# Weight gathers held over a phase border, multiplications tied to their own phase, and a new order of attention's steps

## The chip, the core and the metric

The kernel runs on one core of a Trainium2 chip. That core has five engines, which run their own instruction rows and wait for each other by semaphores: TensorE (PE, matrix products), VectorE (DVE), ScalarE (ACT), GpSimd (POOL) and SyncE (SP), and 16 DMA engines that move data between memory (HBM) and the core's two on-chip memories. The metric is the time of one execution on the device, in microseconds (us), as the median of several executions.

## What is computed

Three layers follow each other; x has 2304 rows of 512 numbers.

```python
# attention: B=4, H=8, S=576, D=64; heads 0-3 a local mask (32 back), heads 4-7 a strided one
scores = where(mask, q @ k.T / sqrt(D), -1e9); scores -= max(scores)
attn = exp(scores); attn /= sum(attn) + 1e-9
x = attn @ v
# layer one: 8 experts, all of them on all rows, weighted by a Sinkhorn-normalized gate
out = sum(P[:, e:e+1] * (relu(x @ w1[e]) @ w2[e]) for e in range(8))   # w1 512x1024, w2 1024x512
# layer two: each row goes to one expert, 288 rows at most to each, best logits first
for e in range(8):
    mask = assigned == e
    out[mask] = relu(x[mask] @ w1[e]) @ w2[e]
```

## The kernel before

Every float32 product is made of float16 products of a high and a low part, three for each, so each weight matrix exists as a high and a low piece.

**Attention** is 32 steps, numbered 0 to 31, each a part of a few heads. A step passes through S (scores, TensorE), M (row maximum and its scale, VectorE, L404 and L405), E (exponential and row sum, ScalarE, L418), N (normalization: `den` on VectorE, L427 and L428, the product on GpSimd), T (transposes, TensorE), O (product with v, TensorE, L459) and X (split of the result into high and low part, ScalarE and VectorE). A string `ORDER`, written by hand, names these parts one after the other: `S0 M0 ... O31`. Between them stand single letters that advance other work by one step: `s` is a side chain that begins with the scale of v (its first four steps are the reductions `vmx`, L343, two for each load `vl` and `vs` of v; then `amax`, `vall`, `vscale`), `W` and `V` prepare the first weights of layer one (`wmx` L527, splits on ScalarE L547 and VectorE L548), `L` and `Y` load q, k and v, `R` loads raw weights, `G`, `H` and `C` belong to the gate and the routing, and `Q` is one unit of layer one's first expert on TensorE (L662, L680). In this stage each engine runs its instructions in the order of that string. The unit `Q` first appears behind X7.

**Layer one** follows from 326 to 1360 us, and to 1594.8 its last expert together with the logits and the first routing of layer two.

**Layer two** has eight phases, one for each expert, written in the function `ffn`. A phase has eight f-units (first matrix, 12 matmuls of 288 columns, L1736), each followed by relu and copy on ScalarE (L1741, L1742: `h2h`) and a split on VectorE (L1743: `h2l`), and then four d-units (second matrix, 24 matmuls, L1786), whose result ScalarE copies to `yt`. Beside that four things are done for the phase that comes next:

- `search`: the cut of the routing is found in steps. VectorE compares (L1379), TensorE counts (`pcnt`, L1385), VectorE compares the count (L1387), TensorE sums (`pany`, L1391), VectorE takes the step (L1394). These steps stand in TensorE's row between the matmuls.
- `load_w2` gathers the next expert's weights in four pieces of 1 MB (numbered 0 to 3: first matrix high and low, second matrix high and low) by indirect DMAs that GpSimd issues (L1608). Three sets of buffers rotate. They lie in old tiles, so that a piece may be called `acc`, `xh`, `xl`, `w1s`, `w2h` or `w2l` in the trace; its source is `wd`. Each piece is tied by a semaphore to the newest ScalarE copy (`self.copied`), which spreads the pieces over the phase: `part(n)` lets one go when at least `GAP` = 3 units have passed.
- `ffn_g` gathers the 288 rows of x in three gathers of 96 (`g`, L1625), also from GpSimd's queue, once the place of each row is known (d = 1). For phases 1 to 5 SyncE then issues three DMA transposes (`xg`, L1639); in the others TensorE transposes. The first f-unit of the next phase needs `xg`.
- `ffn_osc` multiplies one column of the gathered rows by the routing's weight, three operations of 96 x 1 on VectorE (`osc`, L1649). They are written at f = 4 of the phase that uses the rows; `ffn_y`, which multiplies the result, needs them at that phase's end.

In this layer only TensorE runs in the order as written (`MAN2 = {ET.PE}`). On the other engines a scheduler places an instruction where its operands are due, so it can stand earlier than it is written.

## Time and profile before

| | us |
|---|---|
| median of 3 runs (lowest, highest) | 1857.66 (1850.5, 1863.44) |
| the profiled execution | 1857.89 |
| its span on the chip | 1856.1 |
| busy: PE, DVE, ACT, POOL | 1786.5 (96%), 1126.2, 908.0, 550.6 |

The span is the time from the first to the last instruction of the profiled execution; 1.8 us lie outside of it. Phases of layer two are named by number: phase p starts with its first matmul of L1736, at 1594.76, 1629.43, 1664.11, 1698.46, 1730.03, 1764.80, 1793.19 and 1819.06 us; "1 to 2" is the end of phase 1, where the x rows and weights of phase 2 are fetched. A wait in the profile is the time in which an engine stood still ahead of an instruction, put down to what came last.

### The profile page before, as it was taken

The page shows a single profiled execution, that of the slowest core. Times are in us where ns is not written, and L with a number is a line of the kernel's source. Part 1 is how long each engine was busy: PE and PEld are TensorE (multiplying, and loading weights), DVE is VectorE, ACT ScalarE, POOL GpSimd, SP SyncE. Part 2 cuts the span into 40 slices and gives each one's busy share as a digit, 9 for nine tenths or more (in the row PEclk, how much of TensorE's full clock was granted, in tenths as well). Part 3 has the DMA queues.
Part 4 walks back from the last instruction along what each step waited for, and adds up shares of the span by engine and source line. Part 5 has one row for each costly group of instructions (what it writes and reads, how often), then busy time and mean ns, then how long its engine had stood idle before and what let it go on. Part 6 is the DMA issues. An engine that isn't in the chain of part 4 may idle for free.

```text
span 1856.1 us, 33029 instructions
## 1 busy us (share of the span) xinstructions
PE 1786.5 (96%) x12789; PEld 1087.5 (59%) x12789; DVE 1126.2 (61%) x2706; ACT 908.0 (49%) x2147; POOL 550.6 (30%) x557
## 2 busy tenths in 40 slices
PE   6899999999999999999999999999999999889897
PEld 5666765555455545555555555555546764667786
DVE  5744448767766475646646664677545658767640
ACT  5555533572476347545735654467635540223243
POOL 2121203141343044213413231233355622223341
PEclk8899999999999999999999999999999999999999
DMA  8121012233375047404751553355541213466661
GB/s 266 40 71 41 26 46 80 80 131 120 121 245 191 16 155 249 137 35 159 236 155 52 185 164 106 136 199 173 173 137 45 47 46 117 126 154 197 192 198 61
DMA packets 116561, 237.16 MB, mean 128 GB/s; under 512 B 48620, under 2 KB 53300, under 8 KB 108180
## 3 DMA queue, kind: packets, MB, share of 16 engines
q1 hardware_dynamic: 108724, 192.05, 32.4%
q0 software_dynamic: 7680, 43.01, 6.9%
q8 instruction: 100, 1.64, 0.4%
q14 instruction: 57, 0.47, 0.1%
HBM read 160.75 MB, written 64.50 MB: 121 GB/s over the span
## 4 chain that ended last, share of the span: by engine, by line
PE 57%; issue 15%; DVE 14%; DMA 6%; ACT 5%; POOL 3%; SPq 0%; POOLq 0%; ACTq 0%; DVEq 0%
PE l L1104 22%; PE l L1160 15%; PE l L680 7%; PE l L662 4%; PE mm L1736 3%; DVE w1s L548 2%; PE mm L1786 2%; POOL raw L1013 2%; DMA g<-xd,raw 2%; ACT sm L418 1%; DMA raw<-in_moe_w_dram 1%; DVE w1s L1379 1%; DVE wmx L1060 1%; PE po L459 1%; PE ps L393 1%
## 5 line engine op out<-in xcount | busy, mean ns | idle before, releaser
L1104 PEld LDWEIGHTS <-w1s 128*128 128x128 f16 x3864 | 370.1, 98 | 210.9 <-issue 4.2
L1104 PE MATMUL l<-sx,w1s 128*128 128x384 f16 (+2 forms) x2208 | 337.3, 312 | 1.3 <-ACT vV L1119 1.1
L1160 PE MATMUL l<-w2h,hl 128*128 128x512 f16 x864 | 327.5, 379 | 0.0
L1160 PE MATMUL l<-w2l,hh 128*128 128x512 f16 x864 | 327.5, 379 | 0.0
L1160 PE MATMUL l<-w2h,hh 128*128 128x512 f16 x864 | 327.5, 379 | 0.0
L552 POOL TENSOR_TENSOR m2l<-raw,m2h 128x512 f16<-128x512 f32 x176 | 206.0, 1172 | 395.7 <-ACT raw L551 340.6
L1160 PEld LDWEIGHTS <-hh 128*128 128x128 f16 x1728 | 167.7, 98 | 197.4
L1104 PE MATMUL l<-xh,w1s 128*128 128x384 f16 (+2 forms) x1104 | 258.7, 312 | 3.5 <-DVE hl L952 2.0
L712 DVE SCALAR_TENSOR_TENSOR acc<-l,pe,acc 128x512 f32<-128x512 f32 x126 | 94.2, 749 | 174.2 <-PE l L1160 150.7
L1013 POOL TENSOR_TENSOR raw<-raw 128x256 f32<-128x256 f32 x112 | 100.6, 901 | 324.2 <-DVE w1s L548 244.9
L1060 DVE TENSOR_REDUCE wmx<-raw 128x1 f32<-128x512 f32 x240 | 152.0, 678 | 43.8 <-DMA raw<-in_moe_w_dram 41.7
L1104 PE MATMUL l<-xl,w1s 128*128 128x384 f16 (+2 forms) x552 | 171.3, 312 | 0.0
L550 ACT ACTIVATE m2h<-raw,wscale 128x512 f16<-128x512 f32 x176 | 125.3, 712 | 86.0 <-DVE wscale L288 29.0
L1160 PEld LDWEIGHTS <-hl 128*128 128x128 f16 x864 | 84.5, 98 | 101.9
L1119 ACT ACTIVATE vV<-l 128x384 f32<-128x384 f32 x144 | 68.3, 487 | 133.2 <-PE l L1104 132.3
L551 ACT ACTIVATE raw<-raw,wscale 128x512 f32<-128x512 f32 x176 | 127.0, 722 | 5.7
L680 PE MATMUL l<-w2h,hl 128*128 128x512 f16 x288 | 109.8, 381 | 0.0
L680 PE MATMUL l<-w2l,hh 128*128 128x512 f16 x288 | 109.8, 381 | 0.0
L680 PE MATMUL l<-w2h,hh 128*128 128x512 f16 x288 | 109.8, 381 | 0.0
L429 POOL TENSOR_TENSOR sm<-sm,den 96x768 f32<-96x768 f32 (+1 forms) x32 | 42.7, 1333 | 190.2 <-DVE den L428 118.8
L548 DVE SCALAR_TENSOR_TENSOR w1s<-raw,wscale,w1s 128x512 f16<-128x512 f32 x96 | 82.5, 904 | 17.3 <-ACT w1s L547 17.3
L547 ACT ACTIVATE w1s<-raw,wscale 128x512 f16<-128x512 f32 x96 | 57.8, 658 | 71.8 <-POOL raw L1013 53.9
(399 smaller groups left out, 3009.1 us busy)
## 6 DMA issues: line engine op xcount, KB each, us to landing
raw<-in_moe_w_dram SPq DMA_DIRECT2D x120, 512.0 KB, 5.7
sx<-sd SPq DMA_DIRECT2D x15, 1536.0 KB, 7.4
wd<-m2h SPq DMA_DIRECT2D x64, 256.0 KB, 3.6
wd<-m2l SPq DMA_DIRECT2D x64, 256.0 KB, 3.4
kq<-in_qk_dram SPq DMA_DIRECT2D x16, 592.0 KB, 3.9
sd<-sx SPq DMA_DIRECT2D x3, 1536.0 KB, 5.6
acc<-in_moe_w_dram SPq DMA_DIRECT2D x2, 2048.0 KB, 10.3
w1s<-wl SPq DMA_DIRECT2D x4, 896.0 KB, 5.7
```

What stands on the lines that cost most here:

```text
L548: nc.vector.scalar_tensor_tensor(lo, raw, s, hi, op0=OP.mult, op1=OP.subtract)
L550: nc.scalar.activation(hi, raw, AF.Copy, scale=s)
L551: nc.scalar.activation(raw, raw, AF.Copy, scale=s)
L552: nc.gpsimd.tensor_tensor(lo, raw, hi, op=OP.subtract)
L662: nc.tensor.matmul(ps, l[:, d, fs], r[:, d, t0:t0 + nb], start=k == 0, stop=k == 3 * DC - 1)
L680: nc.tensor.matmul(ps, l[:, f, js], r[:, f], start=k == 0, stop=k == 3 * FC - 1)
L712: self.last = [nc.vector.scalar_tensor_tensor(a, ps, pe[:, c:c + 1], a, op0=OP.mult, op1=OP.add).ins]
L1013: nc.gpsimd.tensor_tensor(o, x, y, op=OP.subtract)
L1060: nc.vector.tensor_reduce(mx[:, 2 * q + k:2 * q + k + 1], part(q)[:, k * 512:k * 512 + 512], axis=AX.X, op=OP.max, apply_absolute_value=True)
L1104: self.nc.tensor.matmul(ps, self.w1s[:, fs, x, k, d], a[y][:, d], start=first and m == 0, stop=m == 5, skip_group_check=not first)
L1119: copy = lambda o, i: nc.scalar.activation(o, i, AF.Copy)
L1160: nc.tensor.matmul(ps, l[:, f, js], r[:, f], start=k == 0, stop=k == 3 * FC - 1)
```

## The change

1. The string `ORDER` has the same parts in another order. At the start S0 and M0 now stand ahead of the first `s`; three `s` stand together ahead of E1; the last `W` ahead of the first unit moves from before T6 to behind X7. Later the exchanges are small.
2. `att_consts` makes ScalarE compute the exponential of one column of ones (`warm`), which nobody reads.
3. Each osc multiplication gets a dependency without a semaphore (it only binds the scheduler) on the `h2l` split of f = 4 of its own phase.
4. `ffn` keeps a list of (phase, piece). What is left of it when the d-units begin is let go there only if it belongs to this phase, or is piece 0 or 1 of the next one, except for one that may go at d = 0; the rest is held over and let go in the f-units of the next phase. Where the next phase's list is made early (f of 3 or less), `GAP` stays 3, else it is 2. The fourth piece of every phase from 1 to 7 thus comes behind the copy of f = 0 of its own phase; before, it was tied to a d-unit or the last f-unit of the phase before. In phases 5 to 7 the pieces 0, 1 and 2 are tied to the units f = 3, 6 and 7 of the phase before, where it was 0, 3 and 6.

```diff
-ORDER = ("s S0 M0 S1 s M1 E0 N0 E1 S2 M2 W s N1 s s L T0 s S3 M3 s E2 s N2 s s S4 M4 O0 W E3 L X0 T1 N3 S5 W W M5 O1 W "
+ORDER = ("S0 M0 S1 s M1 E0 s s s E1 S2 N0 M2 W L N1 s T0 E2 S3 O0 L s s M3 s s S4 s N2 M4 W E3 R X0 T1 N3 S5 W W M5 O1 W "
...
-         "E8 N8 W X5 W T6 O6 X6 T7 s O7 L X7 Q S9 M9 Y Q s E9 Q s T8 s L Q Q s N9 V S10 M10 s Q O8 V V E10 X8 Q T9 Q "
+         "N8 W X5 T6 L O6 X6 s T7 s O7 X7 W Q Q S9 M9 Y s Q T8 E9 s Q L Q Q s N9 V S10 M10 s s Q s O8 V V E10 Q T9 X8 "
...
+        warm = self.asm.tile([128, 1], F32, name="warm")
+        nc.scalar.activation(warm, self.onesf[:, 0:1], AF.Exp)
...
         for s in range(3):
-            self.nc.vector.tensor_tensor(self.fx[ph][1][:, s:s + 1], self.gs[ph][s][:, 2 * DM:].bitcast(F32),
-                                         self.places[ph][1][:96], op=OP.mult)
+            st = self.nc.vector.tensor_tensor(self.fx[ph][1][:, s:s + 1], self.gs[ph][s][:, 2 * DM:].bitcast(F32),
+                                              self.places[ph][1][:96], op=OP.mult)
+            self.tc.add_manual_dep(st.ins, self.split.name, mybir.DependencyInfo(
+                mybir.DependencyClass.NoSync, mybir.DependencyReason.DATA), reason="later")
...
-        parts, since = [], 0
+        parts, since, gap = [], 0, GAP
...
-            if parts and since >= GAP:
-                self.load_w2(ph + 1, (parts.pop(0),), self.copied)
+            if parts and since >= gap:
+                p, k = parts.pop(0)
+                self.load_w2(p, (k,), self.copied)
                 since = 0
...
-                nc.vector.tensor_tensor(hl[:, f], r, hh[:, f], op=OP.subtract)
+                self.split = nc.vector.tensor_tensor(hl[:, f], r, hh[:, f], op=OP.subtract).ins
...
-                        parts, since = list(range(4)), GAP
+                        since = since if parts else GAP
+                        gap = GAP if f <= GAP else GAP - 1
+                        parts += [(ph + 1, k) for k in range(4)]
                         loaded = True
                 part(1)
             yt = self.fy[ph] = fp.tile([128, DC, CAP], F32, name="yt")
+            while parts and parts[0][0] == ph:
+                part(GAP)
             for d in range(DC):
-                part(2)
+                if not d or parts and parts[0][1] < 2:
+                    part(2)
+                else:
+                    since += 2
...
-            while parts:
+            while parts and parts[0][1] < 2:
                 part(GAP)
```

The row of VectorE at the program's start, before and then after (`vmx` is the reduction of v, `mx` the row maximum of a step, `den` the row sums, `wmx` a maximum of the weights):

```order
L310 CAST identb<-identf 128x128
L343 TENSOR_REDUCE vmx<-vl 128x1
L404 TENSOR_REDUCE mx<-ps 96x2x3
L405 TENSOR_SCALAR mx<-mx 96x2x3
L343 TENSOR_REDUCE vmx<-vl 128x1
L404 TENSOR_REDUCE mx<-ps 96x2x3
L405 TENSOR_SCALAR mx<-mx 96x2x3
L427 TENSOR_SCALAR den<-den 96x2x3
L428 RECIPROCAL den<-den 96x2x3
```

```order
L312 CAST identb<-identf 128x128
L406 TENSOR_REDUCE mx<-ps 96x2x3
L407 TENSOR_SCALAR mx<-mx 96x2x3
L345 TENSOR_REDUCE vmx<-vl 128x1
L406 TENSOR_REDUCE mx<-ps 96x2x3
L407 TENSOR_SCALAR mx<-mx 96x2x3
L345 TENSOR_REDUCE vmx<-vl 128x1
L345 TENSOR_REDUCE vmx<-vs 72x1 x2
L429 TENSOR_SCALAR den<-den 96x2x3
L430 RECIPROCAL den<-den 96x2x3
```

The first row maximum now stands ahead of the reduction of v that waits for the load, and all four reductions stand ahead of the first `den`, where it was two.

The row of GpSimd's queue in phase 4, before and then after; `wd_73` to `wd_76` are the sources of pieces 0 to 3, and the `w1s`, `w2h` and `w2l` rows are the pieces for phase 5:

```order
L1608 DMA w1s<-wd_73,raw_3214 128x4096
L1704 DMA out_dram<-y,raw_3214 2304x512 x2
L1608 DMA w1s<-wd_74,raw_3214 128x4096
L1704 DMA out_dram<-y,raw_3214 2304x512
L1608 DMA w2h<-wd_75,raw_3214 128x4096
L1608 DMA w2l<-wd_76,raw_3214 128x4096
L1625 DMA g_18957<-xd,raw_3214 96x1026
L1625 DMA g_18959<-xd,raw_3214 96x1026
L1625 DMA g_18961<-xd,raw_3214 96x1026
```

```order
L1610 DMA acc<-wd_76,raw_3216 128x4096
L1708 DMA out_dram<-y,raw_3216 2304x512 x2
L1610 DMA w1s<-wd_73,raw_3216 128x4096
L1708 DMA out_dram<-y,raw_3216 2304x512
L1610 DMA w1s<-wd_74,raw_3216 128x4096
L1610 DMA w2h<-wd_75,raw_3216 128x4096
L1627 DMA g_18958<-xd,raw_3216 96x1026
L1627 DMA g_18960<-xd,raw_3216 96x1026
L1627 DMA g_18962<-xd,raw_3216 96x1026
L1610 DMA w2l<-wd_76,raw_3216 128x4096
```

The fourth piece for phase 5 (`w2l`) moved behind the three x gathers, and the fourth piece for phase 4 (`acc<-wd_76`) now opens the phase.

The row of VectorE in the second matrix of phase 4, before, and then of VectorE in the first matrix of phase 5, after; the `jt` rows and those with `pcnt` and `pany` are the search:

```order
L1379 SCALAR_TENSOR_TENSOR w1s<-w1s,zero,jt_2445 128x400
L1379 SCALAR_TENSOR_TENSOR w1s<-w1s,zero,jt_2445 128x320
L1649 TENSOR_TENSOR osc<-g_18957,raw_3214 96x1
L1387 TENSOR_SCALAR w1s<-pcnt,sx 128x40
L1649 TENSOR_TENSOR osc<-g_18959,raw_3214 96x1
L1394 TENSOR_SCALAR w1s<-pany,zero 128x40
L1649 TENSOR_TENSOR osc<-g_18961,raw_3214 96x1
```

```order
L1748 TENSOR_TENSOR h2l<-h_19253,h2h 128x288
L1553 TENSOR_TENSOR sx<-w1s,raw_3216 128x864
L1492 CAST raw_3216<-raw_3216 128x2
L1748 TENSOR_TENSOR h2l<-h_19284,h2h 128x288
L1651 TENSOR_TENSOR osc<-g_18958,raw_3216 96x1
L1651 TENSOR_TENSOR osc<-g_18960,raw_3216 96x1
L1651 TENSOR_TENSOR osc<-g_18962,raw_3216 96x1
```

The three osc rows of phase 5 left the search steps of phase 4 and stand in phase 5, behind a split.

## Rows read from the trace of the kernel before

**Rows 1.** Windows by stage: stretch, length, busy us (instructions), granted clock, DMA share, GB/s

```profile
58.00:253.00 195.00, 192.11 (x1960) 135.35 (x1960) 92.79 (x236) 104.94 (x442) 36.76 (x38) 0.97 0.13 43
...
326.00:1360.00 1034.00, 1029.85 (x5627) 541.27 (x5628) 654.24 (x1216) 570.60 (x1069) 314.32 (x292) 1.00 0.45 148
...
1594.80:1841.10 246.30, 229.37 (x2403) 186.33 (x2403) 135.92 (x619) 83.52 (x185) 69.14 (x70) 0.97 0.57 166
```

**Rows 2.** Windows by half phase of layer two (first, second matrix)

```profile
1609.30:1629.43 20.13, 16.38 (x211) 13.10 (x209) 11.77 (x49) 2.49 (x6) 5.55 (x6) 1.00 0.82 233
1629.43:1643.13 13.70, 13.70 (x130) 11.37 (x131) 12.13 (x64) 7.69 (x17) 4.98 (x5) 1.00 0.39 121
1643.13:1664.11 20.98, 15.93 (x212) 12.88 (x209) 11.04 (x39) 2.49 (x6) 5.14 (x5) 0.96 0.89 209
...
1680.55:1698.46 17.91, 16.08 (x216) 13.09 (x212) 10.14 (x37) 2.24 (x6) 4.96 (x5) 1.00 0.84 231
...
1712.21:1730.03 17.82, 15.88 (x212) 13.01 (x210) 9.35 (x34) 2.08 (x5) 5.29 (x5) 1.00 0.75 224
...
1743.73:1764.80 21.07, 16.93 (x212) 13.64 (x209) 9.51 (x36) 2.08 (x5) 4.49 (x5) 0.92 0.72 186
```

**Rows 3.** Waits of TensorE in layer two: us in total, times, longest

```profile
PE pany L1391 <- DVE w1s L1387: 7.6, 5, 4.1
PE pcnt L1385 <- DVE w1s L1379: 4.0, 8, 0.9
PE mm L1736 <- DMA xg<-g: 3.9, 1, 3.9
```

**Rows 4.** Waits of VectorE in layer two, same columns

```profile
DVE osc L1649 <- DMA g<-xd,raw: 23.3, 14, 5.2
```

**Rows 5.** Timeline, phase 4: start, us, engine, line, operation, [idle <- releaser]

```profile
1748.29 0.92 POOL L1625 DMA_INDIRECT g<-xd,raw  x1 [2.16 <-DVE raw L1561]
...
1756.77 0.16 DVE L1649 TENSOR_TENSOR osc<-g,raw 96x1 f32<-96x1 f32 x1 [5.22 <-DMA g<-xd,raw]
```

**Rows 6.** The three x gathers of phase 4 to 5, by tile g

```profile
DMA to landing us min/median/max: 7.7/8.1/8.5
```

**Rows 7.** The three x gathers of phase 1 to 2, by tile g

```profile
DMA to landing us min/median/max: 3.1/3.4/4.1
```

**Rows 8.** Timeline of GpSimd's queue, phase 1

```profile
1653.21 0.96 POOL L1608 DMA_INDIRECT w2l<-wd,raw  x1 [0.30 <-issue]
```

**Rows 9.** The three transposes of phase 1 to 2, by tile xg

```profile
L1639 SPq DMA_TRANSPOSE xg<-g x3: 1212/1213/1914, 1652.5 to 1655.4; - x3
...
DMA to landing us min/median/max: 4.1/8.6/9.4
```

**Rows 10.** Transposes of 2 to 3 and 3 to 4, by tile xg

```profile
DMA to landing us min/median/max: 2.7/3.3/3.9
```

**Rows 11.** Windows behind TensorE's two longest stops, columns as in rows 1

```profile
1662.30:1669.10 6.80, 4.99 (x38) 3.35 (x39) 1.51 (x8) 0.85 (x2) 0.00 (x0) 0.50 0.14 27
1757.90:1761.30 3.40, 3.40 (x32) 2.41 (x30) 1.26 (x4) 0.00 (x0) 0.00 (x0) 0.50 1.07 121
```

**Rows 12.** Timeline at the program's start, all engines

```profile
6.79 1.60 PE L393 MATMUL ps<-kq 64*96 64x128 f32 x12 [1.86 <-DMA kq<-in_qk_dram]
...
12.86 0.95 DVE L343 TENSOR_REDUCE vmx<-vl 128x1 f32<-128x768 f32 x1 [11.09 <-DMA vl<-in_vl_dram]
...
14.96 1.28 ACT L418 ACT_TABLE_LOAD   x1 [14.96 <-DVE mx L405]
...
16.25 0.36 ACT L418 ACTIVATE sm<-ps,mx 96x128 f32<-96x128 f32 x1
```

**Rows 13.** Window of attention's first steps, columns as in rows 1

```profile
24.40:52.20 27.80, 20.61 (x272) 16.81 (x272) 24.47 (x57) 26.32 (x125) 10.21 (x9) 0.92 0.68 220
```

**Rows 14.** Timeline of TensorE, first unit of layer one

```profile
57.96 0.40 PE L662 MATMUL l<-xh,w1h 128*128 128x256 f16 x1
```

**Rows 15.** The weight gathers of layer two, by line L1608

```profile
DMA to landing us min/median/max: 5.7/7.1/9.4
```

More of the change, by code (lines that the diff above doesn't have):

```diff
@@ L30 @@
 KQ_BUFS, SM_BUFS, P_BUFS = 3, 3, 2
-ORDER = ("s S0 M0 S1 s M1 E0 N0 E1 S2 M2 W s N1 s s L T0 s S3 M3 s E2 s N2 s s S4 M4 O0 W E3 L X0 T1 N3 S5 W W M5 O1 W "
[11 rows of a table removed]
+ORDER = ("S0 M0 S1 s M1 E0 s s s E1 S2 N0 M2 W L N1 s T0 E2 S3 O0 L s s M3 s s S4 s N2 M4 W E3 R X0 T1 N3 S5 W W M5 O1 "
[11 rows of a table added]
 WM = "aaaaaaaa"
```

21 rows, old and new, of the table ORDER are left out of this document.

## The prediction

> **What bounds the kernel now.** I first read the windows by stage [rows 1]. TensorE is busy 1029.85 of the 1034 us from 326 to 1360, and 192.11 of 195 from 58 to 253: an edit there can only gain what keeps TensorE from starting, and the change adds or removes no matmul. From 1594.8 to 1841.1, layer two, it is busy 229.37 of 246.3, at a granted clock of 0.97, with 16.9 us idle. The windows by half phase [rows 2] say where: the second matrix of phases 0 to 4 has 3.75, 5.05, 1.83, 1.94 and 4.14 us idle, together 16.7; the other eleven half phases have none to speak of (13.70 of 13.70 in the one shown).
>
> Then the waits [rows 3, 4]. TensorE waits 7.6 us at `pany` for the search step L1387 of VectorE, 4.0 at `pcnt` for L1379, 3.9 for the transposed x rows. VectorE in turn sat 23.3 us at `osc` (L1649) for a gather of x rows, 5.2 at the longest. So most of what looks like search is a chain: gather g, then osc, which stands among the search steps of VectorE's row, then the step behind it, then `pany` on TensorE.
>
> The two large places were read in the timeline. In 4 to 5 the x gathers go out at 1748.29, behind two weight pieces on GpSimd's queue, and osc ends a wait of 5.22 at 1756.77 [rows 5]; these gathers landed after 7.7 to 8.5 us [rows 6], those of 1 to 2 after 3.1 to 4.1 [rows 7]. In 1 to 2 the last piece goes out at 1653.21 [rows 8], among the three transposes (1652.5 to 1655.4), which land after 4.1, 8.6 and 9.4 us [rows 9]; with no weight gather in flight they need 2.7 to 3.9 [rows 10]. After both stops TensorE runs at 0.50, its lower level, for 4.99 and 3.40 busy us [rows 11].
>
> At the program's start the other engines set the end: VectorE's first step, a v reduction, waits until 12.86 for the v load, and the first row maximum, whose scores were done at 6.79 + 1.60 = 8.39, stands behind it; ScalarE's table load starts when that maximum is there, at 14.96, takes 1.28, and the first exponential follows at 16.25 [rows 12]. From 24.4 to 52.2 ScalarE is busy 26.32 of 27.80 us and VectorE 24.47 [rows 13]. The first unit of layer one starts at 57.96 [rows 14].
>
> **Part 1, the tied multiplications.** Fourteen waits at osc, 23.3 us of VectorE, cost nothing by themselves; what counts is what stood behind them. Moved behind the split of f=4 of their own phase, they come some 8 us after the transposes of the same rows, which TensorE needs at f=0; the gathers have landed by then. Of the 16.7 us idle I put down to osc or late x rows the 7.6 of `pany`, the 3.9 of xg and, of the 4.0 of `pcnt`, 3.1, the stops that follow an osc [rows 3]: 14.6. The 3.9 is the transposes' and the rest osc's. 2.1 remain, VectorE's own pace. What is late next is VectorE itself: in the first half of a phase it is busy 12.13 of 13.70 us [rows 2], and three operations of 0.16 [rows 5] enter it; 0.5 in each of seven phases would be 3.4 at most if nothing hid it. In phases 5 to 7 nothing is searched any more, and f=4 is behind the search's thick part, so I take zero.
>
> **Part 2, the held-over piece.** Per phase the same four gathers of 1 MB are issued. The fourth now goes out behind the first unit of its own phase. In 1 to 2 this takes the piece from among the transposes, so they should land within 3.9 [rows 10], the last at 1655.4 + 3.9 = 1659.3. TensorE reached phase 2 at 1664.1 − 3.9 = 1660.2 and comes about 1 earlier without its `pany` stop of that phase (5.05 idle, less 3.9); I charge 0.7. In 2 to 3 and 3 to 4 the piece stood between the x gathers, and now stands behind them; TensorE waited for osc alone there, charge 0.3. In 4 to 5 both late pieces stood ahead of the x gathers; now one does, but the held piece of the phase before has taken the first place, so the third goes out only some 1.8 us earlier, by the order and the ends of the units that release it. The gathers then land at about 1755 instead of 1756.7; the third transpose goes out 2.9 behind the first [rows 9] and takes 2.7 to 4.1: 1760.6 to 1762. TensorE, without its stop of 4.14 and the 1.7 of half clock behind it, reaches phase 5 not at 1764.8 but at 1759.0. I take a wait of 2.3. In 0 to 1, 0.2. Given back: 3.5.
>
> Clock: without the two stops, 4.99/2 = 2.5 and 3.40/2 = 1.7 come back [rows 11], if the granted clock then stays up as in the phases without a stop of over 2 us. So layer two gains 14.6 − 3.5 + 4.2 = 15.3; the ends are 10 (the waits at 4 to 5 stay, without the clock's 1.7, and 3.4 of osc's cost is only partly hidden) and 18.8 (nothing given back).
>
> On the gathers behind weight pieces the Trainium skill, "DMA: Bandwidth & Descriptors", section "Queues, rings and completion order", says that an engine turns from queue to queue at packet borders but takes one ring in its order. By that the transposes would share with a piece, as [rows 9] show (twice the time, not more), while an x gather behind a piece on GpSimd's own queue waits for all of it, as [rows 6] show beside [rows 7]; it speaks against a full gain in 4 to 5, and the sum without the 2.3 would be 17.6.
>
> **Part 3, the start of attention.** M0 needs only S0 once the v reduction stands behind it, and the table load leaves the path. From the end of the v reduction to the table load, maximum and scale took 14.96 − 13.81 = 1.15 [rows 12]; from 8.39 on that gives a first exponential at about 9.6, 6.6 earlier. That much doesn't come through. Three reductions that were spread over VectorE's first steps (0.95 and more each) [rows 12] now stand before the first den, and VectorE and ScalarE are nearly full until 52.2 [rows 13]: their work has to be done before the first unit. By stepping the new order with the old durations, E2 and M5 come 2.0 to 2.9 us earlier. One preparing operation on ScalarE, some 0.7, leaves the way of T6. The first unit, which waits for the X7 split, starts 2.7 to 3.6 earlier; I take 2.8, with 0 and 5.8 as bounds. After 58 TensorE is busy without a gap, so a start earlier is an end earlier. The exchanged steps in 253 to 1360 have TensorE's full row ahead of them: zero; one wait of the size that is there now (2.9 in the 195 us) is within the range.
>
> The Trainium skill, "ScalarE: Activation LUTs", section "What ACT_TABLE_LOAD costs", gives 1.28 us for the load and 1.38 for a drain, 2.66 together. The load's 1.28 agrees with [rows 12], and the exponential starts right at its end, with no drain. By the page, 1.4 more would come off; the sum goes by the row.
>
> **The sum.** 15.3 + 2.8 = 18.1. The profiled execution took 1857.89, 1.8 more than its span, and the median of the three runs is 1857.66, so either base gives 1839.8: **1840 us**, 1.0% faster.
>
> **Rivals.**
> (1) The x rows stay late. Each phase moves the same 4 MB, and the x gathers still follow weight pieces on one queue. Then only the short stops behind osc go, in phases 0, 2 and 3: 3.75 + 1.83 + 1.94 − 2.1 = 5.4 [rows 2], and the two long ones come back as a wait for xg at the phase border, with the half clock behind them. With the 2.8: 8.2, 1849.7 us. For it: gathers of 7.7 to 8.5 [rows 6]. Against it: in 1 to 2 the gathers were quick [rows 7], and only the piece at 1653.21 slowed what followed. Chance 0.25. This is also what the page on queues would give if it ruled every phase, and the trace bears it out for one phase of five.
> (2) Nothing is given back, and the start comes through nearly whole: 18.8 + 5.8 = 24.6, 1833 us. For it: 4 to 5 is the only place where two pieces precede the x gathers. Against: full VectorE at the start. Chance 0.17.
> (3) Slower: the held piece comes too late. Each phase begins its second matrix 13.7 us after its start (1629.43 to 1643.13) [rows 2], and needs the fourth piece there. It is issued behind the first unit's copy: units take 13.7/8 = 1.7, the copy another one at most, so at 3.0 to 3.4; it has 10.3 us. Weight gathers landed in 5.7 to 9.4 [rows 15]. If the x rows' transposes and the writes out push a landing over 10.3, each us costs 7, once in each phase; the gain of 18.1 is gone at 12.9, and at 15.5 the time is 1876. Against it: the slowest landing before is 9.4. Chance 0.04.
> (4) The stops only change their names, and nothing measurable is left: 1857, chance 0.05, since the bounds of part 2 and of part 3 would both have to fall at their low ends.
>
> **How the numbers follow.** The forecast has 0.49, rival 1 0.25, rival 2 0.17, rival 3 0.04, rival 4 0.05. The forecast's own range is 1833 to 1847 (10 to 18.8, with 0 to 5.8 taken together). The range of 8 in 10 is 1831 to 1851: it takes in rivals 1 and 2 but for their outer ends, and leaves out 3 and 4. One per cent of 1857.66 is 18.6 us, about what a measurement here can tell from no change (the three runs lie 13 us apart), so faster means under 1839.1. Rival 2 lies there, nearly half of the forecast, and none of rival 1: 0.17 + 0.24 = 0.41. Within 1%: 0.55. Slower: 0.04.
>
> **What the profile after would show.** VectorE's osc waits nearly gone, from 23.3; `pany` and `pcnt` waits of TensorE down from 11.6 to under 5; the second halves of phases 0, 2 and 3 within 1 us of idle; in 1 to 2 transposes landing within 4.5; in 4 to 5 a wait of 1 to 4 for xg, not for VectorE; the fourth piece landing 6 to 9.5 us after its issue and no weight load waiting for it; first exponential at 9 to 11, first unit at 54 to 56. The prediction is wrong if the x rows come late at more than one border, if a weight load waits at the second matrix, or if the first unit stays at 58.

## The result

The changed kernel takes 1839.79 us (median of 6 runs, 1837.8 to 1843.98), the kernel before 1853.49 (median of 6, 1850.5 to 1863.44). The ratio is 0.9917, with a 95% interval of 0.9898 to 0.9937. The profiled execution took 1837.8 us with a span of 1836.0: 20.1 us less than the profiled execution of before, of which the medians bear out 13.7. More executions of the kernel before, run beside the experiments in four sets of 15 to 31, have medians of 1852.47 to 1854.78; the one execution on which the prediction was built, 1857.89, lies 3 to 5 us above these.

The windows of the changed kernel (columns as in [rows 1]): the whole of layer two, and the second matrices of phases 0 to 4, which answer to [rows 2].

```profile
1587.68:1825.01 237.33, 228.45 (x2477) 187.67 (x2477) 135.47 (x619) 84.80 (x189) 71.77 (x71) 1.00 0.55 173
1601.86:1620.24 18.38, 15.91 (x211) 13.03 (x209) 11.11 (x43) 2.09 (x5) 4.61 (x5) 1.00 0.68 198
1633.94:1651.27 17.33, 15.62 (x212) 12.89 (x210) 10.26 (x37) 2.09 (x5) 4.55 (x5) 1.00 0.79 200
1665.43:1682.88 17.45, 15.60 (x215) 12.87 (x212) 10.41 (x34) 2.50 (x7) 3.91 (x4) 1.00 0.65 195
1696.77:1713.53 16.76, 15.88 (x211) 13.00 (x211) 8.94 (x31) 2.09 (x5) 4.70 (x5) 1.00 0.64 197
1727.23:1744.56 17.33, 15.98 (x211) 12.93 (x209) 10.15 (x36) 2.50 (x6) 4.41 (x5) 1.00 0.69 197
```

Layer two lasted 250.4 us before (1594.76 to its last matmul at 1845.16) and lasts 237.3 now, at a granted clock of 1.00. TensorE's idle time in the five second matrices fell from 16.7 to 2.47 + 1.71 + 1.85 + 0.88 + 1.35 = 8.3 us. The half clock behind the two long stops [rows 11] is gone.

TensorE's waits in layer two, against [rows 3] (the lines have moved down by 2 to 5):

```profile
PE pany L1393 <- DVE w1s L1389: 5.5, 7, 1.1
PE pcnt L1387 <- DVE w1s L1381: 1.5, 4, 0.8
PE mm L1741 <- DMA xg<-g: 0.6, 1, 0.6
```

The `pany` waits fell only from 7.6 to 5.5 and are seven small ones now; the longest is 1.1 where it was 4.1. VectorE's 23.3 us of waiting for gathers at osc [rows 4] have no row any more.

The program's start, all engines, against [rows 12]: the table load at 0.80, the first exponential, the first v reduction, those of `vs`, the first maximum of the weights, and the reciprocal that yields the scale of v.

```profile
0.80 1.28 ACT L310 ACT_TABLE_LOAD   x1 [0.80 <-PEq L2038]
...
8.90 0.36 ACT L420 ACTIVATE sm<-ps,mx 96x128 f32<-96x128 f32 x1 [6.60 <-DVE mx L407]
...
11.00 0.95 DVE L345 TENSOR_REDUCE vmx<-vl 128x1 f32<-128x768 f32 x1 [2.20 <-DMA vl<-in_vl_dram]
...
14.37 2.34 DVE L345 TENSOR_REDUCE vmx<-vs 72x1 f32<-72x1024 f32 x2 [0.51 <-DMA vs<-in_vs_dram]
...
19.56 1.22 DVE L529 TENSOR_REDUCE wmx<-acc 128x1 f32<-128x1024 f32 x1 [0.90 <-DMA acc<-in_moe_w_dram]
...
23.59 0.16 DVE L288 RECIPROCAL vscale<-vscale_i 128x1 f32<-128x1 f32 x1
```

And the first unit of layer one, against [rows 14], in the timeline of TensorE:

```profile
54.12 0.39 PE L664 MATMUL l<-xh,w1h 128*128 128x256 f16 x1
```

The first exponential came 7.35 us earlier, the first unit 3.84. The rest of the 20.1 in this pair of profiles: 13.1 in layer two, and 3.2 between the first unit and layer two (1533.6 us instead of 1536.8), where the change reorders steps of attention and adds no work for TensorE. There the profile of before shows 13.7 us at half clock and the one after 6.8, and half of the difference, 3.4, is as much as that. These stretches come and go with the execution: in the profiles below, from 62 to 1585 us, the half clock lasts 3.4 to 13.7 us, whatever the kernel.

### The profile page after: what moved, and what is told of

It is laid out like the page before. It is cut to its first block, busy times and chain, and to the rows that moved or that the text cites. A ratio compares the mean times of both kernels' runs of the same rounds, so it can differ in the third digit from the quotient of the medians.

```text
span 1836.0 us, 33029 instructions
## 1 busy us (share of the span) xinstructions
PE 1779.1 (97%) x12789; PEld 1084.3 (59%) x12789; DVE 1124.6 (61%) x2706; ACT 908.4 (49%) x2148; POOL 553.1 (30%) x557
## 4 chain that ended last, share of the span: by engine, by line
PE 61%; issue 15%; DVE 12%; ACT 4%; DMA 4%; POOL 3%; SPq 0%; POOLq 0%; ACTq 0%; DVEq 0%
PE l L1106 23%; PE l L1162 15%; PE l L682 7%; PE l L664 4%; PE mm L1741 3%; PE mm L1798 3%; DVE w1s L550 2%; POOL raw L1015 2%; DMA raw<-in_moe_w_dram 1%; DVE w1s L1381 1%; PE po L461 1%; DMA wd<-m2h 1%; DVE wmx L1062 1%; ACT sm L420 1%; PE pcnt L1387 1%
## 5 line engine op out<-in xcount | busy, mean ns | idle before, releaser
L1062 DVE TENSOR_REDUCE wmx<-raw 128x1 f32<-128x512 f32 x240 | 152.0, 678 | 46.9 <-DMA raw<-in_moe_w_dram 46.7
```

The lines of the kernel that those rows point to most:

```text
L1062: nc.vector.tensor_reduce(mx[:, 2 * q + k:2 * q + k + 1], part(q)[:, k * 512:k * 512 + 512], axis=AX.X, op=OP.max, apply_absolute_value=True)
```

## The experiments

Because single executions differ by several us, lengths of a stage are taken from each kernel's one profile, and ratios from the timed runs. Each ratio is to executions of the kernel before that ran beside that kernel, so that it, and not the difference of two medians of the table, says how two kernels compare.

| kernel | median us | ratio to before (95%) | layer two, us | first unit at |
|---|---|---|---|---|
| before | 1853.49 | | 250.4 | 57.96 |
| the change | 1839.79 | 0.9917 (0.9898 to 0.9937) | 237.3 | 54.12 |
| osc tied, alone | 1852.61 | 0.9994 (0.9975 to 1.0013) | 248.6 | 56.68 |
| fourth piece held over, alone | 1845.38 | 0.9956 (0.9937 to 0.9975) | 240.4 | 57.10 |
| both | 1841.70 | 0.9934 (0.991 to 0.9959) | 236.3 | 57.80 |
| both, piece let go at the third d-unit | 1843.41 | 0.9942 (0.9923 to 0.996) | 236.7 | 58.26 |
| osc tied, fourth piece 128 KB | 1845.44 | 0.9954 (0.9937 to 0.9971) | 237.7 | 56.82 |
| order of attention and early exponential | 1852.37 | 0.9987 (0.9969 to 1.0005) | 250.2 | 54.41 |
| order alone | 1854.71 | 0.9995 (0.9978 to 1.0011) | 251.2 | 54.91 |
| early exponential alone | 1850.64 | 0.9985 (0.9966 to 1.0004) | 250.4 | 56.53 |
| the change, piece 3 units later | 1875.60 | 1.0117 (1.0095 to 1.0139) | 272.4 | 56.05 |
| the change, piece 1 unit later | 1846.89 | 0.9961 (0.9944 to 0.9978) | 242.0 | 55.70 |
| the change, reductions behind the first N | 1839.45 | 0.9916 (0.9895 to 0.9936) | 236.8 | 54.67 |
| the change, weight load first | 1837.88 | 0.9907 (0.9886 to 0.9928) | 236.6 | 54.50 |

The code of layer two is that of before in four of these, and its length there is 250.2 to 251.2: much steadier than the totals. The stops inside are not: the second matrix of phase 3 took 17.8 us in the profile of before, 20.7 with the new order and 21.4 with the order alone, that of phase 0 20.1 and (early exponential alone) 22.3. Which gather comes too late changes, the sum stays: the idle time of the five second matrices together is 16.7 to 17.8 us in these four.

**The multiplications tied, alone** (part 3 of the change):

```diff
-            self.nc.vector.tensor_tensor(self.fx[ph][1][:, s:s + 1], ...
+            st = self.nc.vector.tensor_tensor(self.fx[ph][1][:, s:s + 1], ...
+            self.tc.add_manual_dep(st.ins, self.split.name, ... NoSync ...)
```

> The kernel before with the osc multiplications tied to their own phase and nothing else. Theory A (the stops of TensorE are two chains: short ones through osc and the search, and the late transposes of 1 to 2 and late x gathers of 4 to 5, which osc cannot mend): the short stops of phases 0, 2 and 3 shrink by about 3 us together, the stop of 3.9 for xg in 1 to 2 stays and grows to 4 to 5, and the 4.14 at pany in 4 to 5 comes back as a wait for xg of 2 to 4; layer two 3 to 5 us shorter, ratio 0.997 to 0.999. Theory B (osc in the search is the whole cause, and the transposes follow it): layer two 11 to 14 us shorter, ratio about 0.993.

Layer two is 1.9 us shorter, the time not to be told from no change. Windows of layer two and of the second matrices of phases 1 to 4:

```profile
1594.63:1843.18 248.55, 231.75 (x2477) 188.99 (x2477) 135.87 (x619) 84.93 (x189) 71.01 (x71) 0.98 0.54 165
1642.62:1663.30 20.68, 15.78 (x211) 12.82 (x209) 11.11 (x38) 2.50 (x6) 5.49 (x6) 0.98 0.81 211
1680.18:1699.40 19.22, 16.08 (x217) 13.03 (x212) 10.18 (x35) 2.23 (x6) 4.86 (x5) 1.00 0.72 214
1713.30:1731.79 18.49, 15.72 (x211) 12.94 (x211) 10.42 (x39) 2.49 (x6) 5.67 (x6) 1.00 0.82 235
1745.56:1762.75 17.19, 15.57 (x211) 12.79 (x209) 10.38 (x37) 2.50 (x6) 4.29 (x5) 1.00 0.76 230
```

TensorE's waits in layer two of the same kernel:

```profile
PE mm L1738 <- DMA xg<-g: 6.1, 3, 3.3
PE pany L1391 <- DVE w1s L1387: 5.8, 6, 2.3
```

The second matrix of phase 4 lost its stop (21.07 to 17.19 us; 19.5 to 20.1 in the three other kernels with the old layer two), but phases 2 and 3 are no shorter (19.22 and 18.49), the five together are idle for 16.2 us, and the waits for the transposed x rows rose from 3.9 to 6.1, three times instead of once (the other three kernels show 2.6 to 5.4). Freed of osc, the search no longer waits for x rows; TensorE does, at the next border. The longest `pany` wait left, 2.3 in phase 0, has no gather ahead of it in VectorE's row, and the profile doesn't name what ended it. Theory B, that osc is the whole cause, falls; theory A put too much on osc as well.

**The held-over piece, alone** (part 4): the diff of `ffn` without the tie.

> The kernel before with the fourth weight piece held over the border, and osc left among the search steps. Theory A: the transposes of 1 to 2 land within 5 us and the stop of 3.9 with the half clock behind it goes (about 6 us); in 4 to 5 the x gathers land some 2 us earlier, and the stop at pany shrinks from 4.1 to 2 or so, with or without its half clock (2 to 4 us); the short stops behind osc stay; layer two 6 to 10 us shorter, ratio 0.995 to 0.997. Theory B: no more than 2 us, ratio 0.999.

Layer two 10.0 us shorter, ratio 0.9956, both where theory A puts them. The windows' row of layer two, and VectorE's wait at osc (us in total, times, longest):

```profile
1591.34:1831.72 240.38, 231.32 (x2477) 189.02 (x2477) 135.82 (x619) 84.99 (x189) 71.22 (x71) 0.99 0.55 170
```

```profile
DVE osc L1649 <- DMA g<-xd,raw: 14.5, 11, 5.1
```

VectorE still waits 14.5 us for gathers at osc. Two of these waits, 1.6 and 5.1, lie behind phase 4, where nothing is searched any more; among the search steps there are nine, 7.8 us in all and 2.8 at the longest, where the kernel before has twelve, 16.8 and 5.2. TensorE feels little of them: its idle time in the second matrix of phase 4 is 1.2 us where it was 4.1. The wait of 2.8, in phase 0, is followed by one of 1.7 of TensorE.

**Both edits of layer two**, with the old start:

> Both edits of layer two on the kernel before, without the new order of attention and the early exponential. Theory A: layer two as in the changed kernel, 237 to 238 us instead of 250.4, start of layer one at 58 as before; ratio 0.993 to 0.995, that is 9 to 13 us. If the scheduler's other rows moved with the attention order and carry part of the gain, layer two stays over 240.

236.3 us, as in the changed kernel; the attention edits carry nothing of layer two. That is 4.1 us less than with the held piece alone, 2.0 of them idle time. The second matrix of phase 0 alone makes 4.2 (18.3 us for 22.5), and there the profile of the held piece alone also has 6.8 us of half clock where this one has 3.4. The ratios of the two kernels, 0.9956 and 0.9934, have intervals that overlap, so what the tie adds to the held piece isn't shown by the time.

**The fourth piece behind the x rows, but in the old phase** (the edit against the kernel with both):

```diff
-                if not d or parts and parts[0][1] < 2:
-                    part(2)
+                if parts and (d == 3 or parts[0][1] < (2 if d else 3)):
+                    part(GAP if d == 3 else 2)
```

> Both edits of layer two, but the fourth piece is let go behind the third d-unit of the old phase, some 4 us before its end, instead of behind the first unit of the new one. On GpSimd's queue it stands behind the three x gathers in both. Theory Q (what counts is that the x gathers don't stand behind the piece on their queue): layer two as with the held-over piece, 236 to 238 us, ratio 0.993 to 0.994. Theory A (the piece also slows the transposes while it is in flight): transposes of 6 to 9 us in 1 to 2 and 3 to 4, TensorE stops for xg of 2 to 4 there and 1 or so elsewhere, some with half clock behind: layer two 242 to 248, ratio 0.996 to 0.999.

236.7 us: the piece need not cross the border, it only has to stand behind the x gathers. In 1 to 2 it went out 2.1 us behind the last transpose (1655.08 after 1652.98) and TensorE did not wait for xg. Theory Q holds. The part of theory A that a piece in flight slows transposes was not put to a real test by this kernel, since the piece went out behind the last of them. The other profiles bear on it: in 1 to 2 the slowest transpose landed after 7.2 to 9.4 us in the five kernels that issue the whole piece among the transposes, after 6.0 with 128 KB there, and after 3.9 to 5.0 in the seven that hold it over.

**The fourth piece of 128 KB**, in the place that it had before, with osc tied. The kernel leaves out the rest of that piece. The edit (the target is cut to `n` columns too; with the view that the edit makes of the source, the 128 rows of 1 KB lie one behind the other there):

```diff
+            n = 512 if k == 3 and ph > 1 else 4096
-                                              in_=self.wd[k],
+                                              in_=self.wd[k].rearrange("r (a b) -> (r a) b", b=n),
```

> The kernel with the osc multiplications tied and the fourth piece where it was before the change (ahead of, between or right behind the x gathers), but for phases 2 to 7 that gather moves 128 KB instead of 1 MB: 1 KB of each of its 128 rows, the rest of the piece left as it was in the buffer. Rows and waits of GpSimd's queue are the same. Theory Q-bytes (the x rows are late because 1 MB stands ahead of them in the DMA engines): the second matrices of phases 1 to 4 shrink from 20.7, 19.2, 18.5 and 17.2 us to 16.5 to 17.5, the transposes of 1 to 2 land within 5, layer two 239 to 242. Theory Q-issue (the queue's order as such, its issue times of 1.2 us and the waits of the piece for its release): stays at 246 to 249. Phase 0 to 1 has its whole piece in both.

The row of GpSimd's queue is that of the kernel with osc tied alone, word for word but for this size. Layer two 237.7 instead of 248.6. Its windows:

```profile
1594.69:1832.43 237.74, 228.39 (x2477) 187.73 (x2477) 135.61 (x619) 84.80 (x189) 70.92 (x71) 0.99 0.50 149
1642.88:1660.66 17.78, 15.77 (x212) 12.81 (x209) 10.81 (x38) 2.44 (x6) 5.49 (x6) 1.00 0.82 195
1674.82:1692.12 17.30, 15.61 (x216) 12.88 (x213) 10.34 (x34) 2.42 (x7) 4.87 (x5) 1.00 0.64 189
1706.00:1722.73 16.73, 15.89 (x211) 13.01 (x211) 8.95 (x31) 2.08 (x5) 5.66 (x6) 1.00 0.68 205
1736.49:1752.24 15.75, 15.41 (x212) 12.85 (x210) 9.29 (x33) 2.08 (x5) 4.29 (x5) 1.00 0.75 190
```

The second matrices of phases 1 to 4 are about as short as in the changed kernel, that of phase 4 shorter; that of phase 0, beside which the piece is whole in both, has 19.9 us and 19.6 with osc tied alone. The slowest transpose of 1 to 2 took 6.0 us, not 5. In phase 4 the first x gather and the transposes behind it (GpSimd and SyncE in the timeline), with the full piece ahead of them (osc tied, alone) and then with the small one:

```profile
1750.12 0.93 POOL L1625 DMA_INDIRECT g<-xd,raw  x1 [2.16 <-DVE raw L1561]
...
1757.13 3.89 SPq L1639 DMA_TRANSPOSE xg<-g  x3
```

```profile
1741.06 0.92 POOL L1626 DMA_INDIRECT g<-xd,raw  x1 [2.16 <-DVE raw L1561]
...
1745.54 4.75 SPq L1640 DMA_TRANSPOSE xg<-g  x3
```

The transposes follow the gather after 7.0 us with the 1 MB piece ahead, and after 4.5 with 128 KB. So it is the bytes ahead of the x rows, not the place in the row or the waits for its release. The Trainium skill, "DMA: Bandwidth & Descriptors", section "Queues, rings and completion order", has a DMA engine take the descriptors of one ring in its order. The traces agree: 7.0 and 4.5 us with the same row on GpSimd's queue. No run puts the piece on another queue, so that it would have to be this queue isn't shown.

**The order of attention and the early exponential**, together and each alone:

```diff
-ORDER = ("s S0 M0 S1 s M1 E0 N0 E1 S2 ...
+ORDER = ("S0 M0 S1 s M1 E0 s s s E1 S2 ...
+        nc.scalar.activation(warm, self.onesf[:, 0:1], AF.Exp)
```

> The new order of attention with the early exponential, layer two as before. Theory A: first unit of layer one at 54.1 as in the changed kernel, 3.8 us earlier than before, passed through to the end, and layer two as before within 1 us but for its clock: 3 to 5 us, ratio 0.997 to 0.998. Theory C (the exchanged steps after 58 carry something too, since layer two began 7.1 us earlier in the changed kernel): 6 to 8 us, ratio 0.996.

> The new order of attention without the early exponential. If the table load costs its 1.28 us on the path, the first exponential starts at 10.2 (8.90 + 1.28); if a drain stands with it (2.66), at 11.5. Theory A: the load delays the first unit of layer one by 0 to 1.3 against 54.1 to 54.4 with both: 54.1 to 55.7; the order carries 2.5 us or more of the 3.7. Theory B (the early exponential carries it): 57 or later.

> The early exponential on the kernel before. The first row maximum still stands behind the v reduction, which waited until 12.86, so the first exponential starts at 15.0 instead of 16.25; first unit 0 to 1.3 earlier than 56.7 to 58.0 (the range of four profiles with the old order); ratio 0.999 to 1.000, not to be told from no change. Theory B (the early exponential carries the start): first unit at 55.5 or earlier.

With both, the first unit starts at 54.41; with the order alone at 54.91; with the early exponential alone at 56.53, just below what the six other profiles with the old order show (56.68 to 58.26). The times of all three can't be told from no change: the outer ends of their intervals are 0.9966 and 1.0011. Theory C (0.996, something carried behind 58 us) lies outside the interval of the order with the exponential, 0.9969 to 1.0005. The first exponential with the order alone (timeline of ScalarE):

```profile
8.74 1.28 ACT L418 ACT_TABLE_LOAD   x1 [8.74 <-DVE mx L405]
10.04 0.36 ACT L418 ACTIVATE sm<-ps,mx 96x128 f32<-96x128 f32 x1
```

In the six profiles that have the new order and the early exponential it starts at 8.78 to 9.49. With the load on the path it starts 1.30 us behind the load's start, so the load costs its own 1.28 us and nothing besides. What of that reaches the first unit is lost in the spread of the profiles with the new order, 54.12 to 56.05.

**What the start hangs on.** Two kernels were meant to find it. One takes the first row sums ahead of three v reductions:

```diff
-ORDER = ("S0 M0 S1 s M1 E0 s s s E1 S2 N0 M2 W L N1 s T0 ...
+ORDER = ("S0 M0 S1 s M1 E0 N0 E1 S2 M2 s s W s L N1 s T0 ...
```

> The changed kernel with the three v reductions that stand together moved behind the first N: VectorE takes the first row sums before them. Theory A (these reductions hold up the start, as they wait for the v load and stand ahead of the first row sums): the first row sums are taken at 13 to 14 instead of 16.6, and the first unit of layer one starts 1 to 2.5 us earlier than 54.1 to 56.0. Theory L (the start now hangs on VectorE's and ScalarE's full rows and the weight loads behind): first unit at 54 to 56 as now. By time both are about 1838 to 1840, ratio 0.991 to 0.993, too near to tell apart; the trace decides.

The first row sums were taken at 13.21 instead of 16.64, and the first unit came at 54.67: nothing gained. VectorE then stood 2.07 us for the first weight load, until 19.29. So the other moves that load to the front (`gates` holds the two loads for the gate, which `first` issued before):

```diff
-        self.att_load_v(0)
-        first()
+        first()
+        self.att_load_v(0)
+        self.gates()
-ORDER = ("S0 M0 S1 s M1 E0 s s s E1 S2 N0 M2 W L N1 s T0 ...
+ORDER = ("S0 M0 S1 M1 E0 N0 E1 S2 M2 W s s N1 s s L s T0 ...
```

> The changed kernel with the first weight load of layer one issued ahead of the loads of v, the gate's two loads behind v, and all v reductions behind the first N and the first W. Theory L (the first unit hangs on the landing of that load, some 35 us ahead of it): the first maximum of the weights runs at 15 to 17 instead of 19.3 to 20.7, and the first unit starts at 51 to 53; ratio 0.989 to 0.991. Theory V (the scale of v, whose loads now come later, is as late a need): first unit at 54 to 57, ratio 0.991 to 0.993.

Theory L falls by the first unit, 54.50, which is where theory V puts it. VectorE's timeline in this kernel:

```profile
14.35 1.22 DVE L530 TENSOR_REDUCE wmx<-acc 128x1 f32<-128x1024 f32 x1 [0.77 <-DMA acc<-in_moe_w_dram]
...
19.81 2.34 DVE L345 TENSOR_REDUCE vmx<-vs 72x1 f32<-72x1024 f32 x2 [0.78 <-DMA vs<-in_vs_dram]
...
24.01 0.16 DVE L288 RECIPROCAL vscale<-vscale_i 128x1 f32<-128x1 f32 x1
```

The weights' maximum came 5.2 us earlier than in the changed kernel, and the first unit stayed. What held still is the scale of v, at 24.0. The same three of the kernel before:

```profile
21.93 1.21 DVE L527 TENSOR_REDUCE wmx<-acc 128x1 f32<-128x1024 f32 x1
23.05 1.20 DVE L343 TENSOR_REDUCE vmx<-vs 72x1 f32<-72x1024 f32 x1
...
27.77 0.16 DVE L288 RECIPROCAL vscale<-vscale_i 128x1 f32<-128x1 f32 x1
```

In all fourteen profiles the first unit stands 30.2 us behind that reciprocal (old order) or 30.5 (new): 57.96 − 27.77, 54.12 − 23.59, 54.50 − 24.01. Behind the first exponential it stands 41.7 to 46.9. So what sets the first unit has happened by that place of VectorE's row, and the chain of work that leads to the first unit (the view of the profile that follows each step back to what released it: start, us, what) names it. In the changed kernel:

```profile
3.57 10.78 DMA vs<-in_vs_dram
...
14.37 2.34 DVE vmx L345 x2
16.71 0.09 DVE den L429
```

It comes from the second load of v over the two `vs` reductions to the first row sums, and on over GpSimd's product and TensorE's row (transposes, scores, products with v) to the scale of v; the weights' maximum at 19.56, which waited 0.9 us for its load, is not on it. With the row sums ahead of the reductions it comes from the weight load instead, and with that load in front again from the second load of v:

```profile
4.53 14.74 DMA acc<-in_moe_w_dram
```

```profile
4.32 15.47 DMA vs<-in_vs_dram
```

So several loads stand behind the start, one about as late as the other; each kernel removed one wait, and the next one took its place (reciprocal at 23.59, 24.16 and 24.01). The new order moved that reciprocal from 26.3 to 28.0 (seven profiles) to 23.6 to 25.5 (seven). A kernel with the row sums first, both loads of v in front and the weights' maximum behind `amax` would be the next step; it wasn't tried. The kernel with the weight load first is 0.9907 of before, the changed one 0.9917: not to be told apart.

**The fourth piece later.** The changed kernel with it behind f = 3, and behind f = 1:

```diff
+                if f == 0 and parts and parts[0][0] == ph:
+                    held, since = parts.pop(0), 0
+                else:
+                    part(1)
+                if f == 3 and held:          # 1 in the other
+                    self.load_w2(held[0], (held[1],), self.copied)
+                    held = None
```

> The changed kernel with the fourth piece let go three units later (behind f=3 instead of f=0, 5.2 us). It then has 5.6 us to its first use instead of 10.8. Theory A (weight gathers land in 5.7 to 9.4 here too, so the slower ending stands just behind the range): TensorE waits at the second matrix in most of seven phases, 0.1 to 3.8 each, 10 us together at the median of 7.1, some half clock more: 1848 to 1860 us. Theory F (with no x rows in flight a piece lands in under 5.6): nothing, 1840.

36 us slower than the changed kernel; both theories fell short. Waits of TensorE:

```profile
PE mm L1804 <- DMA xl<-wd,raw: 10.1, 2, 5.2
PE mm L1804 <- DMA acc<-wd,raw: 8.3, 3, 5.6
PE mm L1804 <- DMA w2l<-wd,raw: 7.8, 2, 4.1
```

Seven waits, 26.2 us, one at each second matrix of phases 1 to 7, with 33.2 us of half clock in layer two against 1.8. In phase 1 the piece went out at 1634.23, not at the 1631 or so of its release, since writes of y and the next phase's first piece stood ahead in GpSimd's row; that left it 2.6 us to the second matrix at 1636.87, and it was waited for until 1642.75, 8.5 behind its issue. In the seven phases the piece has 1.9 to 5.0 us from its issue to the second matrix, in the changed kernel 10.2 to 11.4.

> The changed kernel with the fourth piece let go one unit later (behind f=1). It then has some 8.7 us to its first use, of 10.4 in the changed kernel. With landings of 5.7 to 9.4, as before: TensorE waits in none to two of the seven phases, under 1 us each: 1839 to 1843. If the pieces land after 8.6 as where they were let go three units later (a wait of 5.6 behind an issue 3.2 before the second matrix): waits of 0 to 0.5 in a few phases. If it loses over 5 us, the changed kernel stands nearer to the edge than the landings say.

7.1 us slower than the changed kernel, layer two 4.7 longer, and no wait for a weight piece in it. So the piece, which has 8.4 us in phase 1 (1628.84 to 1637.28) and 8.8 to 10.1 in the others, was still in time, and the loss of over 5 us does not mean that the changed kernel stands near the edge of the landings. The waits are VectorE's: in phase 1 `pany` waited 2.16 us behind splits and `sx` rows that stood together on VectorE. That the scheduler placed these otherwise because the pieces were tied to another copy is argued, not shown.

## Why the prediction was right, and where not

**The time** fell on the forecast: 1839.8 for 1840, ratio 0.9917 for 0.9905. Two errors cancelled in it. The base was an execution 3 to 5 us above the medians, and the gain of 18.1 lay above the 13.7 of the medians, though within the interval (0.9898 is 18.9 us). That 1840 was hit to the microsecond is luck; that the time would fall within 1833 to 1847 is not.

**Where TensorE loses time**: right. Nearly all that layer two gained is idle time of the second matrices and half clock.

**Part 1, the chain through osc**: the step that failed. It put 10.7 of 14.6 us to osc, since osc was the last link ahead of `pany`. The tie alone gave 1.9 us of layer two and no measurable time. The chain is real, as phase 4 showed (21.07 to 17.19), but its first link is the late gather, and with that unmended the waits went over to xg (3.9 to 6.1). Some of the 14.6 was also the search's own, for which the sum had left 2.1: in the kernel before three of the five `pany` waits, 0.6 and 1.1 in phase 0 and 0.3 in phase 1, come back as 0.6, 1.1 and 0.6 in the changed kernel, and there the search takes 7.6 us in all with no gather among its steps. One of these waits, VectorE and TensorE in the timeline:

```profile
1644.08 0.26 DVE L1389 TENSOR_SCALAR w1s<-pcnt,sx 128x39 bf16<-128x39 f32 x1 [2.06 <-PE mm L1798]
1644.40 0.18 PE L1393 MATMUL pany<-w1s,first 128*128 128x39 bf16 x1 [1.14 <-DVE w1s L1389]
```

The count of this step ends at 1642.5 on TensorE, whose row has six matmuls between it and `pany`, until 1643.26; then both engines stand until VectorE's comparison at 1644.08. So the row has too little work there to cover the step from count to comparison, 1.6 us here. The forecast recovered 14.6 − 3.5 = 11.1 us of idle time, the trace 8.4.

**Part 2, the held-over piece**: right in kind, far too small. It was priced at the 3.9 of 1 to 2 and its clock, less 3.5 given back. Alone it gave 10.0 us of layer two and a ratio of 0.9956, and the small piece shows why: 1 MB ahead of the x rows was the cause of the late gathers too, not of the slow transposes alone. (These were slower than the prediction reads them: 8.6 us at the median against 3.3, [rows 9, 10], is 2.6 times, not twice.) What would be given back was overdrawn, 3.5 for the 0.6 that TensorE now waits for xg. In 4 to 5 two pieces still go ahead of the x gathers, and the held one opens the next phase:

```profile
1726.75 1.08 POOL L1610 DMA_INDIRECT w1s<-wd,raw  x1 [2.55 <-PE pany L1393]
1728.58 1.05 POOL L1610 DMA_INDIRECT w2h<-wd,raw  x1 [0.76 <-ACT h2h L1747]
1731.89 0.93 POOL L1627 DMA_INDIRECT g<-xd,raw  x1 [2.26 <-DVE raw L1563]
...
1747.51 1.14 POOL L1610 DMA_INDIRECT w2l<-wd,raw  x1 [12.24 <-ACT h2h L1747]
```

The transposes start 6.2 us behind the first gather (SyncE's timeline):

```profile
1738.12 4.72 SPq L1641 DMA_TRANSPOSE xg<-g  x3
```

They are late as forecast; TensorE was late enough itself to wait 0.6 and not 2.3.

**Clock**: 4.2 forecast; layer two gained 13.1 with 8.4 of idle time, which leaves 4.7 of shorter busy time. Half clock in layer two went from 12.9 us to 1.8; 0.9 of the difference is the end of a stretch that began before layer two, with which the change has nothing to do.

**Part 3, the start**: 2.8 forecast, 3.8 in the pair of profiles, 2.2 between the medians of five profiles with the new string (54.12 to 56.05, median 54.91) and seven with the old (57.10), 2.4 by the ratio 0.9987, whose interval takes in nothing and 5.7. Right in size, and right that most of the 6.6 of the first exponential would be lost. The reason given, full engines and reductions ahead of the first row sums, was half of it: the chain of the changed kernel does run over these reductions, but with the row sums ahead of them nothing was gained, since the loads of the weights and of v set the same time. For the table load the Trainium skill, "ScalarE: Activation LUTs", section "What ACT_TABLE_LOAD costs", gives 1.28 us and a drain of 1.38 more. The traces agree on the first and show no drain: load at 8.74, exponential at 10.04.

**Rival 1** (x rows stay late): refuted by the waits of the changed kernel, 0.6 us for xg in all. **Rival 2** (nothing given back) was right on the giving back and wrong on the size. **Rival 3** (the held piece too late): it has 10.4 us in phase 1 (1623.54 to 1633.94) and TensorE waited for none, as forecast. Its price was set too low: three units later it cost 36 us, 26 of waits for the piece and the rest mostly half clock, which the estimate of 7 us for each us left out. **Rival 4** (nothing measurable) falls with the interval.

**The signs.** Met: osc's waits and every wait for a weight piece are gone, and the first unit stands at 54.12. Missed: `pany` and `pcnt` came to 7.0 us instead of under 5, the second matrices of phases 0 and 2 still idle for 2.5 and 1.9 instead of 1, the transposes of 1 to 2 landed within 5.0 instead of 4.5, TensorE waited 0.6 for xg in 4 to 5 instead of 1 to 4, and the first exponential came at 8.90, just ahead of 9. When the fourth piece landed, the trace of the changed kernel doesn't tell.

## What to carry to other kernels

Ask of a chain of waits which link began late, not which one stands last: untying the last link handed the wait on (1.9 us of layer two), and moving one transfer of 1 MB behind three small ones on the same queue removed it (10.0 us). Put small gathers that somebody needs next ahead of bulk ones that have time, and read from the trace how much time these have: here 10.4 us were enough, and 8.4 still, while 1.9 to 5.0 cost 36. Take the base of a forecast from the median, and the lengths of stages, which are steadier, from more than one profile where there are some.

## What the runs showed that was not expected

The half clock in a part of the program that doesn't change comes in stretches of 3.4 or 6.8 us, one to three of them from 62 to 1585 us, near the same few places (about 125, 250, 305 and 1530 us) in some profiles and not in others. TensorE had been busy for 10.0 of the 10 us before those near 1530 and for 9.0 to 9.9 before those near 125 and 250. Each costs 1.7 or 3.4 us where TensorE is busy. With the granted clock of the whole execution goes just under half of the spread between runs of one kernel (a correlation of 0.68 between the time and the clock lost, over the 86 executions of the kernel before beside the experiments, 1844.75 to 1865.5 us); what makes the rest isn't shown.

The first weight load, issued at 4.16 us behind the loads of q, k and v, was there for VectorE at 19.56; issued ahead of those of v, at 14.35, 5.2 us earlier. The second load of v, which then stood behind it, was there at 19.81 instead of 14.37, 5.4 later. One early load made another late by as much, and the first unit stayed where it was.
